# Attention block with a sine-gated feed-forward: batch 0's x by casting DMAs, and a new order of the opening

## The chip, the cores and the metric

The kernel runs on one core of one Trainium2 chip. The metric is the device time of one execution in microseconds, the median over several runs. TensorE is PE in the profile (PEld is its weight load), VectorE is DVE, ScalarE is ACT, GpSimd is POOL and SyncE is SP.

## The reference

```python
# x: (8, 8, 512, 64), state: (8, 8, 32, 64); scale = 1/sqrt(64)
a  = softmax(scale * x @ state^T)          # per batch and head: 512 x 32
xread = a @ state                          # 512 x 64
a2 = softmax(scale * state @ x^T)          # 32 x 512
sread = a2 @ x                             # 32 x 64
X  = concat([xread, sread], axis=2)        # -> (8 * 544, 512), heads side by side
h  = X @ w_in                              # 512 -> 2048
g  = h + sin(alpha * h)**2 / (alpha + 1e-9)
out = g @ w_out                            # 2048 -> 512, float32
```

Inputs and output are float32 in HBM; the matmuls run in bfloat16.

## The kernel before, in words

The 4352 rows of the output are cut into nine tiles: tile t = 0 to 7 holds the 512 xread rows of batch t, and tile 8 the 256 sread rows of all batches.

For tiles 0 to 7 the product `a @ state @ w_in` is regrouped: `M = state @ w_in` is made per batch (steps `m.b.s`, four column slices s of 512, each with two halves g), copied to bf16 by ACT or DVE (`me`), and multiplied with the transposed softmax weights `AT`. The 2048 hidden columns are 16 blocks f of 128. For each block, PE makes `h` (two matmuls of 512 columns, one for each g: `hg.t.f.g`, or `h.t.f` for both), ACT the sine (`si`), ACT, DVE or POOL its square (`sq`), DVE `gT = s2 / alpha + h` (`gt`), and PE adds gT into four output accumulators st = 0 to 3 (`o.t.st.f0.f1`). `oc` copies an accumulator out of PSUM, `os` stores it from SP.

The softmax weights of a batch come from: the load of x, its transpose xT, scores (`sc`), exponential (`ex`, ACT), row sums and reciprocals (`rs`, `rr`, DVE), the product `nm`, and a transpose of A into AT, by PE (`at`, `ac`) for batch 0 and by a DMA from SP (`ad`) for the later batches. Batch 1's x is transposed by PE (`xt`, `xc`), later ones by DMA (`td`); `pk` copies x into another layout, `xp`.

The order of every engine's work is written out by hand: `ORDER` is a list of steps, `name.arguments`, and each step issues its instructions on its engines in that order. The last numbers of a PE step are its PSUM banks; there are eight, and a step that takes a bank waits until the readers of what was in it are done. Every load of weights and of later batches' x (`li` = w_in slice, `lo` = w_out quarter, `l_st` = state, `lx` = x of a batch) is a DMA from POOL that casts float32 to bfloat16, in one queue. ACT changes its function table when it goes from exponential to sine and back.

The opening deals with batch 0: `lq.0` to `lq.3` load x in four float32 quarters from SP, `xq` casts them on ACT into xp, `xtq` transposes, `xc` copies to xT. Between these steps PE runs `warm_up.n.cols.bank`, matmuls on zeros whose result is not used. `st_t` and `st_c` transpose the state of batches 2 to 7, `s01_t` and `s01_k` that of batches 0 and 1, `al_t` the rows of alpha.

Of the kernel before, what the change touches and what calls it, by code (L numbers as in the profile page):

```python
# [12 lines left out]
BF16 = mybir.dt.bfloat16  # L13
FP32 = mybir.dt.float32
# [7 lines left out]
touch_x l_s01 consts touch lq.0.S ident_ l_alpha lq.1.S zero.0 warm_up.7.512.3 exp_table lq.2.S  # L22
zero.1 identf.V lq.3.S s01_c.G l_st li.0 xq.0.A s01_t.4 li.1 xtq.0.5 warm_up.1.384.3 xq.1.A
s01_k.1.V s01_k.0.A li.2 xtq.1.6 warm_up.2.448.3 xc.0.0.0.V xq.2.A xc.0.0.1.V lo.0 al_t.7 xq.3.A
xtq.2.0 warm_up.1.384.3 al_c inva sc.0.0.1 lo.1 xc.0.1.0.A warm_up.1.256.3 xtq.3.2 warm_up.2.128.3
ex.0.0 warm_up.2.128.4 lx.1.0.1 warm_up.2.128.5 xc.0.1.1.V warm_up.2.128.6 warm_up.2.128.7 rs.0.0
sc.0.1.0 li.3 st_t.0.3 ex.0.1 rr.0.0 st_t.1.4 lo.2 st_c.0.0.V st_c.0.1.A warm_up.2.128.5
warm_up.2.128.6 warm_up.2.128.1 st_c.1.0.A rs.0.1 warm_up.2.128.2 warm_up.2.128.7 nm.0.0.0.4.G
warm_up.2.128.0 warm_up.2.128.5 st_c.1.1.A warm_up.2.128.3 warm_up.2.128.6 warm_up.2.128.1 rr.0.1
warm_up.2.128.2 sin_table warm_up.2.128.7 warm_up.2.128.0 nm.0.1.0.4.G at.0.0.5 warm_up.2.128.3  # L30
ac.0.0.V m.0.0.6.4 m.1.0.1.2 lo.3 at.0.1.7 me.0.0.0.V me.0.0.1.A warm_up.2.128.0 warm_up.2.128.3
me.1.0.1.A ac.0.1.V hg.0.2.0.5 me.1.0.0.V hg.0.1.0.4 hg.0.2.1 hg.0.1.1 hg.0.0.0.0 lx.2.0.1 si.0.2
hg.0.0.1 m.1.1.6.3 si.0.1 m.0.1.7.2 hg.0.3.0.1 me.0.1.1.A sq.0.2.V hg.0.3.1 sq.0.1.G me.1.1.0.V
# [124 lines left out]
class Steps:  # L158
# [505 lines left out]
```

The softmax here doesn't subtract the row's maximum and nothing guards it: scores larger than these inputs give would overflow.

## Time and profile before

| what | us |
|---|---|
| median of 3 runs | 221.14 (220.92 to 221.36) |
| profiled execution (span) | 221.2 |
| PE busy | 215.7 (97%), of which 9.9 are warm-ups |
| ACT, DVE, POOL busy | 173.5, 162.4, 107.1 |
| first sine of tile 0 starts | 16.52 |
| step `h.1.8` starts on PE | 46.06 |

The span runs from the first to the last instruction of the core; the profiled execution agrees with the median within 0.1 us, so times read in the trace can be set against the runs directly. A busy PE in the table includes the modelled ends of pipelined matmuls; the distance from one start to the next is what counts in a stretch without gaps.

### The profile page before, as it was taken

How to read it: one execution, taken by the hardware profiler on the slowest of the kernel's cores; microseconds unless marked ns; L12 is line 12 of the kernel's file. 1: busy time of each engine (PE TensorE's matmuls, PEld its weight loads, DVE VectorE, ACT ScalarE, POOL GpSimd, SP SyncE). 2: the span in 40 equal slices, each digit the busy share in tenths (PEclk: the TensorE clock that was granted, in tenths of full speed). 3: DMA queues.
4: the chain of work that ended last, by engine and by line, in shares of the span. 5: the costliest groups of instructions: out<-in, count | busy, mean ns of one | idle time of the engine just before them, and what ended most of it. 6: DMA issues, size and time to landing. Idle time of an engine off the chain costs nothing.

```text
span 221.2 us, 4330 instructions
## 1 busy us (share of the span) xinstructions
PE 215.7 (97%) x1619; PEld 106.0 (48%) x1619; DVE 162.4 (73%) x286; ACT 173.5 (78%) x297; POOL 107.1 (48%) x115
## 2 busy tenths in 40 slices
PE   7999999999999999999999999999999999999994
PEld 3664454444444444444454444445445555665452
DVE  3468986999678979988888778889766988571201
ACT  3589878998899979998996999798857897685111
POOL 6866626595388728934863377363501072121000
PEclk9999999999999999999999999999999999999999
DMA  6999995953549518375325437380220211012042
GB/s 172 198 206 204 205 203 87 174 199 73 119 127 158 96 50 150 44 190 61 81 41 125 126 95 94 108 117 17 47 99 0 98 47 47 0 50 95 1 142 96
DMA packets 38052, 23.48 MB, mean 106 GB/s; under 512 B 20992, under 2 KB 33680, under 8 KB 38032
## 3 DMA queue, kind: packets, MB, share of 16 engines
q0 software_dynamic: 11648, 8.13, 26.1%
q1 hardware_dynamic: 26128, 15.08, 26.1%
q8 instruction: 12, 0.20, 0.4%
q14 instruction: 8, 0.07, 0.1%
q10 hardware_dynamic: 256, 0.01, 0.1%
HBM read 17.44 MB, written 8.91 MB: 119 GB/s over the span
## 4 chain that ended last, share of the span: by engine, by line
PE 93%; ACT 3%; DMA 2%; SPq 0%; issue 0%
PE o_ps L587 54%; PE h_ps L537 22%; PE m_ps L488 4%; PE h_ps L543 3%; PE h_ps L552 3%; DMA x<-in_x_dram 2%; PE s_ps L399 2%; PE warm_ps L303 2%; PE w_ps L450 2%; PE w_ps L461 1%; PE x_ps L361 1%; ACT L226 1%; ACT s L560 1%; ACT M L496 1%; PE x_ps L376 0%; PE st_ps L333 0%
## 5 line engine op out<-in xcount | busy, mean ns | idle before, releaser
L587 PE MATMUL o_ps<-w_out_sb,gT 128*128 128x512 bf16 (+2 forms) x560 | 137.7, 373 | 0.0
L576 DVE SCALAR_TENSOR_TENSOR gT<-s,inva_sb,h_ps 128x512 bf16<-128x512 bf16 (+1 forms) x144 | 96.6, 714 | 18.8 <-POOL s L201 9.6
L201 POOL TENSOR_TENSOR s<-s 128x512 bf16<-128x512 bf16 (+1 forms) x76 | 76.7, 1021 | 65.9 <-ACT s L560 62.4
L560 ACT ACTIVATE s<-h_ps,alpha_sb 128x512 bf16<-128x512 f32 (+1 forms) x144 | 88.8, 671 | 10.5 <-PE h_ps L543 4.3
L587 PEld LDWEIGHTS <-gT 128*128 128x128 bf16 x560 | 52.3, 98 | 60.3 <-issue 5.0
L537 PE MATMUL h_ps<-AT,M 128*128 128x512 bf16 x224 | 60.8, 379 | 0.0
L537 PEld LDWEIGHTS <-M 128*128 128x128 bf16 x224 | 21.7, 98 | 25.9 <-issue 0.4
L569 ACT ACTIVATE s<-s 128x512 bf16<-128x512 bf16 (+1 forms) x53 | 31.4, 595 | 0.8
L201 POOL TENSOR_TENSOR A<-E,rR 128x512 bf16<-128x512 bf16 x16 | 16.6, 1048 | 25.7 <-ACT o_sb L595 12.7
L595 ACT COPY o_sb<-o_ps 128x512 f32<-128x512 f32 (+2 forms) x24 | 13.7, 571 | 16.6 <-PE o_ps L587 16.5
L496 ACT CAST M<-m_ps 128x512 bf16<-128x512 f32 x35 | 18.6, 594 | 8.2 <-PE m_ps L488 8.1
L496 DVE CAST M<-m_ps 128x512 bf16<-128x512 f32 x29 | 18.9, 679 | 2.5 <-PE m_ps L488 2.1
L595 DVE COPY o_sb<-o_ps 128x512 f32<-128x512 f32 x11 | 7.6, 691 | 13.0 <-PE o_ps L587 12.9
L303 PE MATMUL warm_ps<-warm 128*128 128x128 bf16 (+3 forms) x66 | 9.9, 295 | 1.4 <-DVE warm L209 1.2
L410 DVE TENSOR_REDUCE R<-E 128x16 f32<-128x512 bf16 x16 | 10.4, 658 | 1.1 <-ACT E L406 0.9
L201 DVE TENSOR_TENSOR s<-s 128x512 bf16<-128x512 bf16 (+1 forms) x15 | 6.2, 415 | 6.8 <-ACT s L560 6.7
L488 PE MATMUL m_ps<-w_in_sb,stT 64*32 64x512 bf16 x256 | 10.2, 382 | 0.0
L468 DVE RECIPROCAL rC<-w_ps 128x128 f32<-128x128 f32 x8 | 7.6, 948 | 3.2 <-PE w_ps L461 3.2
L406 ACT ACTIVATE E<-s_ps 128x512 bf16<-128x512 f32 x16 | 8.8, 601 | 1.4 <-PE s_ps L399 1.3
L552 PE MATMUL h_ps<-AT,M 128*128 128x512 bf16 x32 | 9.4, 380 | 0.4 <-ACT M L496 0.4
L543 PE MATMUL h_ps<-xs_all,w_in_sb 128*128 128x256 bf16 x64 | 9.1, 273 | 0.0
L560 ACT ACT_TABLE_LOAD x5 | 6.4, 1283 | 2.2 <-PE h_ps L537 1.1
(56 smaller groups left out, 104.3 us busy)
## 6 DMA issues: line engine op xcount, KB each, us to landing
out_dram<-o_sb SPq DMA_DIRECT2D x33, 256.0 KB, 2.3
xnat<-in_x_dram POOLq DMA_DIRECT2D x7, 512.0 KB, 7.7
w_in_sb<-in_moe_w_in_dram POOLq DMA_DIRECT2D x4, 512.0 KB, 10.3
w_out_sb<-in_moe_w_out_dram POOLq DMA_DIRECT2D x4, 512.0 KB, 16.3
x<-in_x_dram SPq DMA_DIRECT2D x4, 256.0 KB, 4.3
st_nat<-in_state_dram POOLq DMA_DIRECT2D x1, 256.0 KB, 5.7
out_dram<-o_sb SPq DMA_DIRECT2D x1, 192.0 KB, 1.9
s<-in_state_dram SPq DMA_DIRECT2D x1, 128.0 KB, 2.1
```

What stands on the lines that cost most here:

```text
L201: {"V": k.nc.vector, "G": k.nc.gpsimd}[eng].tensor_tensor(out, a, b, ALU.mult)
L303: k.nc.tensor.matmul(wp[:, :cols], k.warm[:, 0:k.P], k.warm[:, :cols], start=True, stop=True)
L488: k.nc.tensor.matmul(k.t["m", b, s + n, g][o0:o0 + k.Ns, :], k.stT[k.half(r), b * k.G + g, c0:c0 + k.Ns], k.w_in_sb[k.half(r), 2 * g + h, ...
L496: k.copy(eng)(k.t["M", b][:, g, s * k.FW:(s + 1) * k.FW], k.t["m", b, s, g][:])
L537: k.nc.tensor.matmul(hp[:, :n], k.t["M", t][:, g, fs], k.t["AT", t][:, g, :], start=(g == 0), stop=(g == k.G - 1),)
L543: k.nc.tensor.matmul(hp[:, :n], k.w_in_sb[:, q, fs], k.xs_all[:, q].rearrange("p b j -> p (b j)"), start=(q == 0), stop=(q == k.Q - 1),)
L552: k.nc.tensor.matmul(k.t["h", t, f][:], k.t["M", t][:, g, f * k.P:(f + 1) * k.P], k.t["AT", t][:, g, :], start=(g == 0), stop=(g == k.G - 1),)
L560: k.nc.scalar.activation(s[:, :n], k.t["h", t, f][:, :n], ACT.Sin, scale=k.alpha_sb[:, f:f + 1])
L569: k.nc.scalar.activation(s2[:, :n], s[:, :n], ACT.Square)
L576: k.nc.vector.scalar_tensor_tensor(gT[:, :n], k.t["s2", t, f][:, :n], k.inva_sb[:, f:f + 1], k.t["h", t, f][:, :n], ALU.mult, ALU.add,)
L587: k.nc.tensor.matmul(k.t["o", t, st, half][:, cols], k.t["gT", t, f][:, rows], k.w_out_sb[:, f, cols], start=(f == 0), stop=(f == k.FT - 1),)
L595: k.copy(eng)(o_sb[:, cols], k.t["o", t, st, half][:, cols])
```

## The change

Of batch 0's x, only the first quarter (heads 0 and 1, `lq.0`) is still loaded in float32 from SP; DVE casts it into the bf16 tile `xnat` (`xn.0`). The other three quarters come as two casting DMAs, the first instructions of POOL's queue: `lx.0.1.4` (heads 2 and 3) and `lx.0.1.2` (heads 4 to 7), ahead of POOL's identity matrix. `xth` transposes x from `xnat` in halves of 64 columns, and xp of batch 0 is made by `pk` on DVE. The loads in POOL's queue stand in the order x0, x0, w_in 0, w_in 1, w_out 0, state, x1, w_in 2, w_out 1, w_in 3, w_out 2, x2, w_out 3; before it was state, w_in 0, 1, 2, w_out 0, 1, x1, w_in 3, w_out 2, 3, x2. The first 312 steps stand in a new order, with 11 warm-up matmuls in place of 66: tile 0's blocks come as f = 0, 1, 2 and so on, batch 0's two `nm` go from POOL to DVE, `s01_c` from POOL to DVE, and `st_t`/`st_c` come after the first `hg` blocks. From `h.1.8` on, the order is that of before with the banks renamed one for one. `hg` now starts an accumulation where a bank is given.

```diff
--- before
+++ after
 ORDER:
-touch_x l_s01 consts touch lq.0.S ident_ l_alpha lq.1.S zero.0 warm_up.7.512.3 exp_table lq.2.S
-zero.1 identf.V lq.3.S s01_c.G l_st li.0 xq.0.A s01_t.4 li.1 xtq.0.5 warm_up.1.384.3 xq.1.A
-s01_k.1.V s01_k.0.A li.2 xtq.1.6 warm_up.2.448.3 xc.0.0.0.V xq.2.A xc.0.0.1.V lo.0 al_t.7 xq.3.A
-xtq.2.0 warm_up.1.384.3 al_c inva sc.0.0.1 lo.1 xc.0.1.0.A warm_up.1.256.3 xtq.3.2 warm_up.2.128.3
-ex.0.0 warm_up.2.128.4 lx.1.0.1 warm_up.2.128.5 xc.0.1.1.V warm_up.2.128.6 warm_up.2.128.7 rs.0.0
-sc.0.1.0 li.3 st_t.0.3 ex.0.1 rr.0.0 st_t.1.4 lo.2 st_c.0.0.V st_c.0.1.A warm_up.2.128.5
-warm_up.2.128.6 warm_up.2.128.1 st_c.1.0.A rs.0.1 warm_up.2.128.2 warm_up.2.128.7 nm.0.0.0.4.G
-warm_up.2.128.0 warm_up.2.128.5 st_c.1.1.A warm_up.2.128.3 warm_up.2.128.6 warm_up.2.128.1 rr.0.1
-warm_up.2.128.2 sin_table warm_up.2.128.7 warm_up.2.128.0 nm.0.1.0.4.G at.0.0.5 warm_up.2.128.3
-ac.0.0.V m.0.0.6.4 m.1.0.1.2 lo.3 at.0.1.7 me.0.0.0.V me.0.0.1.A warm_up.2.128.0 warm_up.2.128.3
-me.1.0.1.A ac.0.1.V hg.0.2.0.5 me.1.0.0.V hg.0.1.0.4 hg.0.2.1 hg.0.1.1 hg.0.0.0.0 lx.2.0.1 si.0.2
-hg.0.0.1 m.1.1.6.3 si.0.1 m.0.1.7.2 hg.0.3.0.1 me.0.1.1.A sq.0.2.V hg.0.3.1 sq.0.1.G me.1.1.0.V
-me.1.1.1.A warm_up.2.128.2 gt.0.2 si.0.0 warm_up.2.128.2 warm_up.2.128.6 warm_up.2.128.3
-warm_up.2.128.2 warm_up.2.128.6 me.0.1.0.A gt.0.1 sq.0.0.G m.0.2.3.2 si.0.3 m.1.2.5.6 hg.0.4.0.7
 ...
-si.1.13 h.1.15.2 sq.1.3.G gt.1.6 os.0.1 o.0.2.15.16 oc.0.0.A h.1.5.4 sq.1.13.G oc.0.2.V si.1.15
-h.1.7.3 os.0.0 gt.1.3 o.1.1.0.1.5 si.1.5 os.0.2 h.1.8.1 sq.1.15.G gt.1.13 o.1.1.1.2 si.1.7
-o.1.2.0.2.7 sq.1.5.A o.1.1.2.3 sq.1.7.G h.1.12.0 gt.1.15 si.1.8 h.1.9.6 gt.1.5 o.1.2.2.3 si.1.12
 ...
+l_s01 lx.0.1.4 touch_x consts lq.0.S touch zero.0 lx.0.1.2 l_alpha exp_table zero.1 ident_ li.0
+identf.V s01_c.V warm_up.4.512.7 warm_up.1.256.6 s01_t.0 li.1 xn.0.V al_t.1 s01_k.1.A s01_k.0.V lo.0
+xth.0.0.2 al_c inva xth.0.1.3 l_st xc.0.0.0.A xc.0.0.1.A lx.1.0.1 warm_up.1.512.0 xth.0.2.4
+xth.0.3.5 li.2 xc.0.1.0.A pk.0.0.V sc.0.0.6 xc.0.1.1.A pk.0.1.V lo.1 ex.0.0 warm_up.1.224.3 sc.0.1.7
+li.3 rs.0.0 ex.0.1 m.0.0.0.1 lo.2 sin_table rr.0.0 rs.0.1 nm.0.0.0.4.V me.0.0.0.A rr.0.1
+warm_up.3.512.6 warm_up.1.320.7 at.0.0.2 nm.0.1.0.4.V me.0.0.1.A m.0.1.3.4 ac.0.0.V at.0.1.5
+me.0.1.1.A me.0.1.0.V hg.0.0.0.6 m.1.0.7.0 ac.0.1.V m.1.1.1.2 me.1.0.1.A me.1.0.0.V hg.0.1.0.4
+hg.0.0.1 me.1.1.0.A hg.0.1.1 me.1.1.1.V hg.0.2.0.3 si.0.0 hg.0.2.1 hg.0.3.0.5 lx.2.0.1 hg.0.3.1
+si.0.1 sq.0.0.V hg.0.4.0.0 hg.0.4.1 si.0.2 gt.0.0 hg.0.5.0.7 lo.3 hg.0.5.1 st_t.0.1 si.0.3 sq.0.1.V
+sq.0.2.G st_t.1.2 si.0.4 gt.0.1 hg.0.6.0.6 st_c.0.0.A st_c.0.1.V hg.0.6.1 sq.0.3.G st_c.1.0.A
+o.0.0.0.1.4 gt.0.2 o.0.0.1.2 st_c.1.1.A hg.0.7.0.1 hg.0.7.1 si.0.5 pk.1.0.V sq.0.4.G xt.1.1.2 gt.0.3
+si.0.6 xt.1.0.3 si.0.7 xc.1.1.0.V sq.0.5.G o.0.0.2.3 gt.0.4 o.0.1.0.1.5 xc.1.1.1.A o.0.1.1.2
+o.0.1.2.3 xc.1.0.0.V sq.0.6.G xc.1.0.1.A o.0.0.3.4 sc.1.1.0 gt.0.5 sq.0.7.A o.0.2.0.1.2 sc.1.0.3
+o.0.2.1.2 pk.1.1.V ex.1.1 o.0.3.0.1.7 gt.0.6 o.0.3.1.2 o.0.2.2.3 o.0.3.2.3 gt.0.7 o.0.1.3.4
+o.0.2.3.4 o.0.3.3.4 m.0.2.6.1 ex.1.0 rs.1.1 o.0.0.4.5 me.0.2.0.A o.0.1.4.5 me.0.2.1.V m.1.2.0.3
+o.0.2.4.5 me.1.2.1.A hg.0.8.0.6 me.1.2.0.V hg.0.8.1 hg.0.9.0.1 si.0.8 hg.0.9.1 rs.1.0 hg.0.10.0.3
+hg.0.10.1 rr.1.1 hg.0.11.0.0 rr.1.0 hg.0.11.1 nm.1.1.0.4.G o.0.3.4.5 o.0.0.5.6 o.0.1.5.6 o.0.2.5.6
+si.0.9 o.0.3.5.6 lx.3.0.1 sq.0.8.V o.0.0.6.7 o.0.1.6.7 si.0.10 gt.0.8 o.0.2.6.7 o.0.3.6.7
+nm.1.0.0.4.G si.0.11 o.0.0.7.8 sq.0.9.V o.0.1.7.8 o.0.2.7.8 sq.0.10.V o.0.3.7.8 sq.0.11.A gt.0.9
+o.0.0.8.9 ad.1 o.0.1.8.9 o.0.2.8.9 gt.0.10 o.0.3.8.9 m.0.3.6.1 o.0.0.9.10 gt.0.11 me.0.3.0.A
+o.0.1.9.10 o.0.2.9.10 me.0.3.1.A o.0.3.9.10 pk.2.0.V m.1.3.3.6 pk.2.1.V hg.0.12.0.0 me.1.3.0.A
+hg.0.12.1 me.1.3.1.V hg.0.13.0.1 td.2 si.0.12 hg.0.13.1 hg.0.14.0.3 hg.0.14.1 si.0.13 hg.0.15.0.6
+sq.0.12.G hg.0.15.1 o.0.0.10.11 si.0.14 o.0.1.10.11 sq.0.13.V o.0.2.10.11 si.0.15 o.0.3.10.11
+gt.0.13 o.0.0.11.12 sq.0.14.G o.0.1.11.12 o.0.2.11.12 gt.0.12 sq.0.15.A hg.1.0.0.1 hg.1.0.1
+o.0.3.11.12 gt.0.14 si.1.0 hg.1.1.0.0 hg.1.1.1 o.0.0.12.13 gt.0.15 si.1.1 hg.1.2.0.3 sq.1.0.G
+hg.1.2.1 o.0.1.12.13 si.1.2 o.0.2.12.13 sq.1.1.V hg.1.3.0.6 hg.1.3.1 gt.1.1 o.0.3.12.13 sq.1.2.A
+o.0.0.13.14 o.0.1.13.14 gt.1.0 si.1.3 o.0.2.13.14 hg.1.4.0.0 hg.1.4.1 gt.1.2 o.0.3.13.14 sq.1.3.G
+si.1.4 hg.1.5.0.1 hg.1.5.1 o.0.0.14.15 si.1.5 hg.1.6.0.3 sq.1.4.V hg.1.6.1 gt.1.3 o.0.1.14.15 si.1.6
+o.0.2.14.15 o.0.3.14.15 o.0.0.15.16 gt.1.4 hg.1.7.0.6 sq.1.6.G oc.0.0.A hg.1.7.1 o.0.1.15.16
+hg.1.13.0.0 os.0.0 oc.0.1.A hg.1.13.1 hg.1.15.0.4 gt.1.6 hg.1.15.1 si.1.13 os.0.1 o.0.2.15.16
+o.0.3.15.16 si.1.15 oc.0.2.V o.1.1.0.1.5 sq.1.13.G oc.0.3.A os.0.2 os.0.3 h.1.8.3 sq.1.15.G gt.1.13
+o.1.1.1.2 si.1.7 o.1.2.0.2.2 sq.1.5.A o.1.1.2.3 sq.1.7.G h.1.12.7 gt.1.15 si.1.8 h.1.9.0 gt.1.5
 ...
...
     def lq(k, q, eng):
-        if q == 0:
-            k.x0 = k.const.tile([k.P, k.H, k.C * k.D], FP32, name="x0")
         hs = slice(2 * q, 2 * q + 2)
+        k.t["x0", q] = k.const.tile([k.P, 2, k.C * k.D], FP32, name=f"x0_{q}")
...
+    def xn(k, q, eng):
+        xnat = k.new(0, "xnat", k.xpool, [k.P, k.H, k.C * k.D], BF16)
+        k.copy(eng)(xnat[:, 2 * q:2 * q + 2, :], k.t["x0", q][:])
...
     def lx(k, b, part, parts):
-        if part == 0:
-            k.t["xnat", b] = k.xpool.tile([k.P, k.H, k.C * k.D], BF16, name="xnat")
+        xnat = k.new(b, "xnat", k.xpool, [k.P, k.H, k.C * k.D], BF16)
         hs = slice(part * k.H // parts, (part + 1) * k.H // parts)
...
-    def xq(k, q, eng):
-        xp = k.new(0, "xp", k.xppool, [k.P, k.C, k.H, k.D], BF16)
-        hs = slice(2 * q, 2 * q + 2)
-        k.copy(eng)(xp[:, :, hs, :], k.x0[:, hs, :].rearrange("p h (i d) -> p i h d", i=k.C))
-
-    def xtq(k, q, bank):
-        tp = k.t["xtq", q] = k.ps(bank, [k.P, k.S], BF16, "x_ps")
+    def xth(k, b, q, bank):
+        tp = k.t["xth", b, q] = k.ps(bank, [k.P, k.S], BF16, "x_ps")
         for i in range(k.C):
-            k.nc.tensor.transpose(tp[:, i * k.P:(i + 1) * k.P], k.pair(0, i, q), k.ident[:])
+            for r in range(2):
+                k.nc.tensor.transpose(
+                    tp[k.half(r), i * k.P:(i + 1) * k.P],
+                    k.t["xnat", b][:, 2 * q + r, i * k.D:(i + 1) * k.D],
+                    k.ident[:],
+                )
...
     def hg(k, t, f, g, *bank):
-        if g == 0:
+        if bank:
...
-            start=(g == 0), stop=(g == k.G - 1),
+            start=bool(bank), stop=not bank,
```

## The prediction

> **What bounds the kernel now.** I read the busy shares first, then the stretches of the span, then the opening in the timeline, then the DMA landings. The stretches (columns: stretch, PE busy and count, PEld, DVE, ACT, POOL, granted clock, DMA share, GB/s):
>
> ```profile
> 16.00:19.40 3.40, 3.17 (x43) 1.37 (x42) 2.15 (x4) 3.21 (x7) 1.04 (x1) 1.00 1.24 206
> 19.40:24.00 4.60, 4.60 (x36) 2.07 (x36) 4.45 (x8) 4.60 (x10) 4.29 (x5) 1.00 1.37 201
> 24.00:46.00 22.00, 22.00 (x156) 10.37 (x154) 18.80 (x34) 18.84 (x31) 11.67 (x12) 1.00 1.08 177
> 46.00:100.00 54.00, 54.00 (x399) 24.69 (x397) 45.93 (x80) 49.06 (x84) 35.11 (x36) 1.00 0.55 113
> 100.00:218.00 118.00, 118.00 (x848) 58.74 (x846) 83.01 (x143) 88.02 (x154) 43.39 (x44) 1.00 0.30 72
> ```
>
> From 19.4 us to 218 us PE never stands still, and in that stretch one 512-column matmul starts every 0.216 us. So every useful matmul that PE has done when it becomes gap-free brings the end forward, and every later gap puts it back. Before 19.4, PE's busy time is mostly filler:
>
> ```profile
> L303 PE MATMUL warm_ps<-warm 128*128 128x128 bf16 (+3 forms) x66 | 9.9, 295 | 1.4 <-DVE warm L209 1.2 <-ACT M L496 0.2
> ```
>
> That is PE's group of warm-ups up to 19.4. The opening's chain in the timeline (start, duration, what):
>
> ```profile
> 4.36 0.62 ACT L356 CAST xp<-x 128x512 bf16<-128x512 f32 x1 [0.69 <-DMA x<-in_x_dram]
> ...
> 8.68 0.64 PE L399 MATMUL s_ps<-stT,xT 128*128 128x64 bf16 x8
> ...
> 10.66 0.40 PE L399 MATMUL s_ps<-stT,xT 128*128 128x64 bf16 x8
> ...
> 11.10 0.60 ACT L406 ACTIVATE E<-s_ps 128x512 bf16<-128x512 f32 x1 [1.15 <-PE s_ps L399]
> ...
> 13.24 1.05 POOL L201 TENSOR_TENSOR A<-E,rR 128x512 bf16<-128x512 bf16 x1 [0.74 <-DVE rR L416]
> ...
> 13.73 1.28 ACT L226 ACT_TABLE_LOAD   x1
> ...
> 16.52 1.26 ACT L560 ACTIVATE s<-h_ps,alpha_sb 128x512 bf16<-128x512 f32 x2 [0.19 <-PE h_ps L552]
> ```
>
> x lands in quarters, ACT casts each, the second exponential ends at 11.7, POOL's second product at 14.29, the first sine starts at 16.52. The two equal groups of s_ps also show PE's rate: 0.64 us at 8.7, 0.40 at 10.7. PE runs at half rate until about 10.5, though the granted clock reads 1.00.
>
> After step `h.1.8` the two orders are the same (banks renamed one for one). Before starts it at 46.06 in the timeline; the end moves by what that start moves. The profiled execution takes 221.2 us, as the median of 221.14, so I subtract from 221.2.
>
> **The landing of x.** Removed: three fp32 quarters on SP and four ACT casts of 0.62. Added: two casting DMAs at the head of POOL's queue, a DVE cast `xn` (0.4 to 0.7 by the 128x512 rows) and two DVE copies `pk.0` (0.42 each, in DVE's wait for the first exponential). The x transposes become 32 of half width instead of 16: eight such took PE 0.64 in the state's group, four whole ones 0.61, so they are even. POOL can issue from 0.74; the two issues take some 0.75 each and push `ident_` to about 2.8, covered by the fillers until 3.2. No row shows this queue used first with a bf16 target of 256 KB, so bounds: the state load of 256 KB, first on the queue before, landed 5.7 after issue; the 512 KB xnat loads landed 5.9 to 8.0 after theirs:
>
> ```profile
> xnat<-in_x_dram POOLq DMA_DIRECT2D x1, 512.0 KB, 8.0
> ```
>
> Queued loads landed every 2.55 us per 512 KB (w_in at 11.6, 14.1, 16.7), 205 GB/s. The state row plus 128 KB (0.6) gives 0.74+5.7+0.6 = 7.05; the xnat rows less 128 KB (0.6) give 6.0 to 8.1. I take 7.05, the row nearest in place and size. Then w_in 0 lands at 9.6, w_in 1 at 12.1, w_out 0 at 14.7, the state at 16.0, x of batch 1 at 18.5, w_in 2 at 21, w_out 1 at 23.6, w_in 3 at 26, w_out 2 at 29.
>
> The Trainium skill, "DMA: Bandwidth & Descriptors", section "Anatomy of one DMA", gives such a load about 2 us plus its bytes at 436 GB/s; by that estimate x would be there before 5 us and the sum below would fall by 0.4 more, where `alpha` takes over. The trace's 5.7 for the state load disagrees, and the sum goes by the trace.
>
> **The chain to the first hidden tile** (durations from the rows; PE at half rate). `al_t` now stands ahead of x on PE; alpha rows landed at 5.2, so `xth.0` 5.3, `xth.1` 5.75. `xth.2` 7.05 to 7.7, `xth.3` to 8.15. ACT: four xT copies 5.95 to 8.8. `sc.0.1` 8.85 to 9.5, second exponential 9.5 to 10.1 (before: 11.7). Sine table 1.5, to 11.6; first M copies to 12.7. DVE: sums 0.68, reciprocals 0.25, and the two `nm` that move from POOL (1.05) to DVE. No row shows that product on DVE; the bf16 one there takes 0.42, POOL's 1.05; I take 0.65, near the 0.68 of rows that read fp32. That ends `nm` at 12.55 (before 14.29). PE: `m.0.0` at 9.6, fillers to 11.65, `at.0.0`, `m.0.1` at 12.15 (w_in 1 at 12.1), `at.0.1` 12.6 to 13.05. First `hg` 13.05 (before 15.11). ACT's five M copies end at 15.2; first sine 15.25 against 16.52.
>
> **From there to h.1.8.** PE work left: 117 matmuls of 512 columns x 0.216 = 25.3; six `m` x 0.3 = 1.8; `st_t` 0.9, `xt` 0.85, `sc` 0.5. Sum 29.35, so 42.4 without a stop. Stops, following ACT (sines every 0.6): sines 0 to 4 until 18.3, three `st_c` (1.46, now here instead of ahead of the tile) until 19.75, sines 5 to 7 until 21.6, xT copies to 22.65, a square to 23.25, exp table 1.28, two exponentials to 25.65, two M copies, sine table to 28.0.
> - half rate until about 14.3: 0.65;
> - `o.0.0` waits for DVE's `gt.0.1` (18.1): 0.05;
> - `hg.0.7` waits for its bank until `st_c` at 18.8: 0.25;
> - `xt.1.1` waits for the last `st_c` at 19.75: 0.5;
> - `sc.1.1`, `sc.1.0` wait for xT copies: 0.5;
> - `m.1.2` waits for the second exponential of batch 1 at 25.65: 0.25.
>
> Sum 2.2: `h.1.8` at 44.6 instead of 46.06, **1.45 us earlier**. The sine table load (to 28.0) is covered: 8 `hg` and 13 `o` (4.5 us) carry PE from 26.2 until tile 0's f=8 is needed at 30.7, and its gT is ready at 29.8. Without that cover it would cost 1.3. Loads have 1 to 7 us: x of batch 1 needed at 19.8, w_out 1 at 25, w_out 2 at 30.7, w_out 3 (31.9) at 37. On POOL, `lx.3` (0.94) stands between batch 1's two `nm` and holds the second to 30.6; `ad.1` (about 3.2 to land) then comes at 34, needed at 36.3. The 55 warm-ups fewer cost PE nothing where it waits anyway.
>
> Forecast: 221.2 - 1.45 = 219.75, rounded to 219.8.
>
> **The clock.** In the trace the half rate ends near 10.5, after a stretch from 7 us nearly full with fillers, transposes and scores. In the new order the same density comes with `m.0.0` and the long fillers at 9.6, hence full rate near 14.3. "TensorE: Matmul & The Clock Gate" in the Trainium skill ("What's actually happening" and Part 4) wants a busy window of about 3.4 us and says that transposes do not count; it speaks against dropping fillers. By it full rate would come only at 16.5 to 19.5 and the sum would lose up to 1.5 us of its gain. No row here separates transposes from fillers. From the trace alone: if half rate lasts to the `o` at 18, eleven `hg` cost 0.216 more each, 2.4 us, of which PE's 1.2 of waits up to 19.8 absorb half: h.1.8 at 45.8, 220.9.
>
> **Rivals.**
> 1. The lead is given back (no change, 220.7 to 221.6). Either the clock case above, or DVE: tile 0's f=8 to 11 are squared on DVE (0.42) with gT (0.66 each), PE reaches `m.0.3` at 31.6 and its bank 1 comes free at 31.2. With DVE 1 us later, PE waits 0.6 there and some again at `hg.0.12`. For: DVE is 97% busy at 19.4 to 24 before. Against: the table of batch 1 comes 3 us earlier than before, so ACT's later stretch is looser.
> 2. Slower: the software queue's first load lands late. From `xth.2` to the first sine each us of lateness is a us of time, w_in 0 and 1 with it. Landing at 8.5 (7.05+1.45) cancels the gain; beyond 8.95 it is measurably slower. For: first packets of this queue before moved only after SP's x; 8.0 from issue is a row. Against: SP now has a third of the bytes ahead. At 9.2, 0.5 past the largest xnat row's 8.7 from 0.74, the time is 221.9.
> 3. The DMA cast brings nothing, since `alpha` or ACT's order holds the chain anyhow: an earlier landing than 6.65 gains no more; then 219.4, the low side.
>
> **How the numbers follow.** Forecast case 0.64 (own range 219.0 to 220.6: landing 6.0 to 7.9 gives -0.4 to +0.8, two `nm` on DVE of 0.42 to 1.05 each give -0.45 to +0.8, not all at once). Given back 0.17, slower 0.19. Range 218.9 to 221.8. 0.2%, 0.44 us, is about what a measurement of this kernel can tell from no change: faster is below 220.7, slower above 221.58. The forecast case reaches 220.6, so faster 0.64, same 0.17, slower 0.19.
>
> **What would show it.** Right: xnat's second load lands at 6 to 8, first sine near 15.3, `h.1.8`'s L537-type matmul near 44.6, PE full from 26 on. Wrong: PE waits for ACT or DVE after 26; 512-column matmuls 0.43 apart after 15; w_in waits at `m.0.1`; or a first xnat landing past 8.5.

## The result, and the profile after

The changed kernel is slower: 229.19 us (median of four runs, 227.61 to 233.19) against 221.03, a ratio of 1.034 [1.028, 1.040]. A second set gave 229.84 against 221.2, 1.037 [1.030, 1.044]. The longest runs, from 232 us up, count as slow executions: they are in the medians and left out of the ratios. The forecast was 219.8, with 221.8 as its upper end.

The profiled execution of after took 227.61 us and has a span of 225.2. The stretches, with the columns as before (us, PE busy and count, PEld, DVE, ACT, POOL, granted clock, DMA share, GB/s):

```profile
16.00:19.40 3.40, 3.40 (x44) 1.83 (x43) 2.69 (x5) 3.40 (x8) 1.65 (x3) 1.00 1.39 202
19.40:24.00 4.60, 4.12 (x51) 2.11 (x50) 4.46 (x8) 3.73 (x8) 4.10 (x4) 1.00 1.24 206
24.00:46.00 22.00, 21.41 (x127) 8.79 (x127) 18.74 (x32) 18.89 (x30) 7.71 (x8) 1.00 0.97 150
46.00:100.00 54.00, 52.24 (x387) 23.58 (x386) 45.45 (x76) 47.23 (x81) 34.35 (x35) 1.00 0.59 113
```

PE was never idle after 19.4 in before. Now this view shows it idle for 0.48, 0.59 and 1.76 us in the last three stretches, most of it after 46 us, where the order of steps is that of before. The view counts the modelled ends of the matmuls as busy; measured from one start to the next, the time lost in stops is larger: 1.36 (19.4 to 24), 0.8 (24 to 46) and 2.3 (46 to 100). What PE waited for from 19 to 100 us (total, times, longest):

```profile
PE s_ps L399 <- DVE gT L576: 1.1, 2, 0.8
PE h_ps L537 <- DVE gT L576: 1.0, 1, 1.0
PE o_ps L587 <- DVE gT L576: 0.3, 1, 0.3
PE h_ps L552 <- DVE gT L576: 0.2, 1, 0.2
```

For before the same view has no line. The chain that ended last, by engine, says the same (before: PE 93%):

```profile
PE 76%; DVE 7%; DMA 7%; ACT 6%; POOL 2%; issue 1%; POOLq 0%
```

The warm-ups are 11 instead of 66, and the opening in the timeline is this (start, duration):

```profile
8.81 0.63 PE L399 MATMUL s_ps<-stT,xT 128*128 128x64 bf16 x8
8.87 1.21 ACT L406 ACTIVATE E<-s_ps 128x512 bf16<-128x512 f32 x2
10.29 0.63 PE L488 MATMUL m_ps<-w_in_sb,stT 64*32 64x512 bf16 x8 [0.84 <-DMA w_in_sb<-in_moe_w_in_dram]
10.85 1.73 PE L304 MATMUL warm_ps<-warm 128*128 128x512 bf16 x4
11.82 0.69 DVE L200 TENSOR_TENSOR A<-E,rR 128x512 bf16<-128x512 bf16 x1
12.37 0.63 PE L430 MATMUL a_ps<-ident,A 128*128 128x128 bf16 x4
16.14 1.28 ACT L560 ACTIVATE s<-h_ps,alpha_sb 128x512 bf16<-128x512 f32 x2
```

The second exponential ends at 10.08, as forecast (10.1). The score groups still take 0.63, PE's half rate, which lasts until 15.53. w_in 0 lands at 10.24 and holds `m.0.0`; the four fillers behind it (1.73 us at half rate) hold the transpose of A until 12.37, although its product was ready at 11.62. The first sine starts at 16.14.

**The profile shown of before was of an execution some 2 us longer than the runs.** The 13 runs of before in the second set have spans of 218.8 to 220.9, and their time is 1.9 us more than their span; by that distance the profile's 221.2 would belong to an execution of about 223. A profile of a typical one (`before_again`, span 219.3, time 221.24) shows the difference in the same places:

```profile
8.34 0.41 PE L399 MATMUL s_ps<-stT,xT 128*128 128x64 bf16 x8
8.79 0.60 ACT L406 ACTIVATE E<-s_ps 128x512 bf16<-128x512 f32 x1 [0.37 <-PE s_ps L399]
14.35 1.26 ACT L560 ACTIVATE s<-h_ps,alpha_sb 128x512 bf16<-128x512 f32 x2 [0.19 <-PE h_ps L552]
```

Full rate comes at 4.86 instead of 10.49, the second exponential ends at 9.39 instead of 11.70, the first sine starts at 14.35 instead of 16.52. So this table compares after with before's order in `old_open_new_tail` below, whose record is complete (us from the span's start):

| point | before's order | after | `no_collisions` |
|---|---|---|---|
| PE at full rate from | 7.02 | 15.53 | 15.81 |
| second exponential ends | 9.84 | 10.08 | 10.18 |
| first sine of tile 0 | 14.67 | 16.14 | 16.35 |
| first output matmul of tile 1 (just ahead of `h.1.8`) | 44.00 | 47.24 | 46.20 |
| first score of batch 2 | 49.18 | 53.42 | 51.47 |
| last matmul | 216.03 | 221.62 | 218.75 |
| span, time of that run | 219.3, 221.23 | 225.2, 227.61 | 222.3, 224.76 |

After loses 1.5 up to the first sine, 1.8 from there to tile 1, 2.3 behind it and 0.3 after the last matmul. Another 0.5 lies outside the span: time less span is 1.9 for before's order and 2.4 to 2.5 for after and `no_collisions`. It is 2.2 in `x_only`, 2.1 in `order_only` and 2.0 to 2.1 in `nc_x_sp` below, so most of the 0.5 goes with the casting loads of x; why, no run here shows.

### The profile page after: what moved, and what is told of

It is laid out like the page before. It is cut to its first block, busy times and chain, and to the rows that moved or that the text cites. A ratio compares the mean times of both kernels' runs of the same rounds, so it can differ in the third digit from the quotient of the medians.

```text
span 225.2 us, 4246 instructions
## 1 busy us (share of the span) xinstructions
PE 215.7 (96%) x1580; PEld 102.8 (46%) x1580; DVE 166.2 (74%) x290; ACT 174.2 (77%) x298; POOL 103.5 (46%) x111
## 4 chain that ended last, share of the span: by engine, by line
PE 76%; DVE 7%; DMA 7%; ACT 6%; POOL 2%; issue 1%; POOLq 0%
PE o_ps L587 45%; PE h_ps L537 16%; PE m_ps L488 4%; DMA xnat<-in_x_dram 4%; DVE gT L576 4%; PE h_ps L543 3%; DMA w_in_sb<-in_moe_w_in_dram 3%; PE h_ps L552 2%; ACT s L560 2%; ACT M L496 2%; PE w_ps L450 2%; DVE xp L348 2%; PE s_ps L399 1%; DVE s L200 1%; PE w_ps L461 1%
## 5 line engine op out<-in xcount | busy, mean ns | idle before, releaser
L200 POOL TENSOR_TENSOR s<-s 128x512 bf16<-128x512 bf16 (+1 forms) x73 | 73.8, 1025 | 68.1 <-ACT s L560 66.8
L537 PEld LDWEIGHTS <-M 128*128 128x128 bf16 x204 | 19.8, 98 | 24.8 <-issue 1.9
L496 ACT CAST M<-m_ps 128x512 bf16<-128x512 f32 x39 | 20.8, 591 | 12.8 <-PE m_ps L488 12.7
L569 ACT ACTIVATE s<-s 128x512 bf16<-128x512 bf16 (+1 forms) x50 | 29.3, 589 | 0.8
L595 ACT COPY o_sb<-o_ps 128x512 f32<-128x512 f32 (+2 forms) x25 | 14.3, 572 | 17.1 <-PE o_ps L587 16.8
L200 POOL TENSOR_TENSOR A<-E,rR 128x512 bf16<-128x512 bf16 x14 | 14.5, 1048 | 27.6 <-ACT o_sb L595 12.9
L496 DVE CAST M<-m_ps 128x512 bf16<-128x512 f32 x25 | 16.3, 678 | 2.9 <-PE m_ps L488 2.8
L200 DVE TENSOR_TENSOR s<-s 128x512 bf16<-128x512 bf16 (+1 forms) x21 | 10.3, 493 | 7.8 <-ACT s L560 7.6
L488 PE MATMUL m_ps<-w_in_sb,stT 64*32 64x512 bf16 x256 | 11.8, 411 | 1.0 <-DMA w_in_sb<-in_moe_w_in_dram 0.8
L348 DVE COPY xp<-xnat 128x1024 bf16<-128x1024 bf16 x16 | 8.5, 557 | 2.3 <-DMA xnat<-in_x_dram 2.3
L276 POOL DMA_DIRECT2D xnat<-in_x_dram x9 | 8.1, 905 | 2.6 <-DMA w_in_sb<-in_moe_w_in_dram 1.8
## 6 DMA issues: line engine op xcount, KB each, us to landing
w_in_sb<-in_moe_w_in_dram POOLq DMA_DIRECT2D x4, 512.0 KB, 11.6
```

Source lines behind the costliest of these rows:

```text
L200: {"V": k.nc.vector, "G": k.nc.gpsimd}[eng].tensor_tensor(out, a, b, ALU.mult)
L348: k.copy(eng)(k.t["xp", b][:, :, hs, :], k.t["xnat", b][:, hs, :].rearrange("p h (i d) -> p i h d", i=k.C),)
L488: k.nc.tensor.matmul(k.t["m", b, s + n, g][o0:o0 + k.Ns, :], k.stT[k.half(r), b * k.G + g, c0:c0 + k.Ns], k.w_in_sb[k.half(r), 2 * g + h, ...
L496: k.copy(eng)(k.t["M", b][:, g, s * k.FW:(s + 1) * k.FW], k.t["m", b, s, g][:])
L537: k.nc.tensor.matmul(hp[:, :n], k.t["M", t][:, g, fs], k.t["AT", t][:, g, :], start=(g == 0), stop=(g == k.G - 1),)
L569: k.nc.scalar.activation(s2[:, :n], s[:, :n], ACT.Square)
```

## The experiments

**Which part costs.** One repeat of after, and three kernels with the change undone in part.

`again`: no edit.

> The changed kernel once more, unchanged. Its runs spread from 227.6 to 233.2 us where those of before stay within 0.8. If the cost sits in DVE copies that start while a POOL product is running (0.42 us becomes up to 1.28), which copies are hit depends on a few tenths of a microsecond, so a second profile shows a different set of stretched copies and a time anywhere from 227 to 233. If the cost is a fixed consequence of the order, the second profile has its gaps at the same steps, within 0.1 us, and the same 225.2 us span.

229.84. The stretched copies are the same as in after, within 0.04 us in length: not chance, but consequence of the order. The new thing is PE's stop ahead of tile 1, 0.38 us in after and 1.08 here, now put down to a DMA (what PE waited for, 19 to 100 us, the three longest):

```profile
PE s_ps L399 <- DVE gT L576: 1.1, 2, 0.8
PE h_ps L537 <- DVE gT L576: 1.0, 1, 1.0
PE h_ps L552 <- DMA AT<-A: 0.9, 1, 0.9
```

`x_only`, on before:

```diff
-touch_x l_s01 consts touch lq.0.S ident_ l_alpha lq.1.S zero.0
+l_s01 lx.0.1.4 touch_x consts lq.0.S touch zero.0 lx.0.1.2 l_alpha ident_
...
-xq.0.A
+xn.0.A
...
-xtq.0.5
+xth.0.0.5
...
-xc.0.1.1.V
+xc.0.1.1.V pk.0.0.V pk.0.1.V
```

`lq.1` to `lq.3` and `xq.1` to `xq.3` are left out, and the other three `xtq` become `xth` likewise.

> Before's order and fillers, and only batch 0's x loaded by the two casting DMAs at the head of POOL's queue (the state and the weights behind them in the order of before). If the new order is what costs, this is within 1.5 us of before (219.5 to 222.5; the second x load lands at 7.1 to 7.2, the second exponential ends about 10.5 instead of 11.7, but w_in 0 lands at 12.8 instead of 11.6 and takes the lead back). If the casting loads are what costs, this is 225 or more.

225.60, 1.019 [1.015, 1.024]: slower by itself, as the second reading had it. In its profile the state lands at 9.58 instead of 8.76 and the first sine comes 0.48 later; 1.68 more is one stop at batch 4's score, whose DMA transpose took 5.9 us instead of 4.3. The profile is of the shortest run (223.88); the others took 225.3 to 226.2, and what they lose beyond it has no trace.

What ran beside that transpose, the trace shows (queues and issues from 70 to 78 us):

```profile
q8 instruction: 1, 0.02, 0.7%
xT<-xp SPq DMA_TRANSPOSE x1, 5.9
```

The same transpose in `old_open_new_tail` below, whose window has no packet of that queue:

```profile
xT<-xp SPq DMA_TRANSPOSE x1, 4.3
```

All 20 traces say the same. Of 131 DMA transposes issued with no casting load in flight, 24 took 0.85 to 1.64 us longer than usual, and in each of the 24 a 16 KB packet of the queue listed as `q8 instruction` starts 1.0 to 3.9 us after the issue. The 99 with no such packet were within 0.3 of the usual, and so were the 8 in which it came only in the first 0.15 or the last 0.3 us. No run moved that packet, so this is a coincidence in time and not a cause shown. The 1.68 cannot be put down to the casting loads themselves.

`order_only`, on after:

```diff
-l_s01 lx.0.1.4 touch_x consts lq.0.S touch zero.0 lx.0.1.2
+l_s01 touch_x consts lq.0.S touch lq.1.S zero.0 lq.2.S lq.3.S
...
-xth.0.1.3 l_st xc.0.0.0.A
+xn.1.A xth.0.1.3 l_st xn.2.A xn.3.A xc.0.0.0.A
```

> The changed kernel with x loaded as before: four fp32 quarters from SP, cast by DVE (first) and ACT (three, 0.6 each); order, fillers and POOL's other loads as in the changed kernel. If the new order is what costs, this stays at 226 to 231. If the loads of x ahead of w_in are what costs, w_in 0 lands about 2.5 us earlier (7.5 to 8) and the time comes back to 219 to 222.

234.75, 1.061 [1.058, 1.065], worse than the changed kernel and outside both readings. POOL's w_in loads now start at 1.43 and share the DMA engines with SP's quarters, which land at 5.4, 9.3 and 11.6 (6.7 for the last in before's order, where POOL starts at 3.3). The four, and the two w_in loads issued beside them:

```profile
x<-in_x_dram SPq DMA_DIRECT2D x4, 256.0 KB, 7.1
w_in_sb<-in_moe_w_in_dram POOLq DMA_DIRECT2D x2, 512.0 KB, 8.6
```

`old_open_new_tail`: before's steps up to `h.1.8`, with banks 0 to 7 become 7, 3, 4, 6, 1, 5, 0, 2, and after's steps from there.

```diff
-os.0.2 h.1.8.1 sq.1.15.G gt.1.13
+os.0.2 h.1.8.3 sq.1.15.G gt.1.13
```

> The steps of before up to h.1.8 (banks renamed) and from there, word for word, the changed kernel's steps. If the changed kernel's loss after h.1.8 comes from the moment at which it arrives there, this is before again: 221.0 within 0.5. If the banks named anew in the rest of the order cost something, it is 222.5 to 224.5, with the gaps that the changed kernel has at sc.2 and at pk.4.

221.25, 1.000 [0.998, 1.003]. The renaming is free; what after loses behind `h.1.8` depends on when and in what state it gets there. So the casting loads cost 4.4 us in before's order (`x_only`), and the new order on top of them 4.2 more (229.84 against 225.60).

**Three candidates, each alone and together**, on after.

`fillers`:

```diff
-warm_up.4.512.7
+warm_up.6.512.7
...
-warm_up.1.512.0
+warm_up.3.512.0
...
-sc.0.1.7
+sc.0.1.7 warm_up.4.512.2
...
-warm_up.3.512.6
+warm_up.6.512.6
```

> The changed kernel with 11 more 512-column fillers on PE in the opening (two more at the start, two more ahead of the second half of x, four between the scores and w_in 0, three more ahead of the transposes of A). If PE's half rate until 15.5 us holds the opening back, full rate now comes at 7 to 10, the first sine at 14.8 to 15.4 instead of 16.14, the first output matmul of tile 1 about 1 us earlier than 47.24, and the time is 1 to 2 us under the changed kernel's 229. If the half rate only fills waits, the first sine stays at 16.0 to 16.5 and the time at 228 to 231; fillers in the way of the transposes would make it later still.

230.45, 1.044 [1.040, 1.048]. Full rate came at 4.14, yet the first sine only at 15.84: w_in 0 landed at 10.90 and the fillers kept the transpose of A until 12.72. PE then stopped 1.8 ahead of tile 1.

`lx4_early`:

```diff
-sq.1.14.G
+sq.1.14.G lx.4.0.1
...
-h.2.3.2 lx.4.0.1 ad.3
+h.2.3.2 ad.3
```

> The changed kernel with the load of batch 4's x moved up in POOL's queue, from 66.1 us to POOL's idle time at 54.6. If PE's stop at 75.7 comes from that load (issued 66.09, landed 74.71, DVE waits 1.43 for it ahead of three gT), the load lands near 63 and the time falls by 1.1 to 1.5; if the load is also what spreads the runs by 5 us (a stop long enough lets the clock drop), the runs now lie within 1.5 us. If the spread comes from the opening, it stays at 4 to 5 us, and only the 1.1 to 1.5 go. If DVE's copy was slow for its own reasons, nothing changes.

229.87, 1.039 [1.035, 1.043]. The stop at 75.7 went (1.13), and a new one came at batch 3's score: its DMA transpose, issued just behind the moved load, took 8.1 us instead of 4.3.

```profile
PE s_ps L398 <- DMA xT<-xp: 1.9, 1, 1.9
```

`pk3_late`:

```diff
-sq.1.12.A pk.3.1.V
+sq.1.12.A
...
-pk.3.0.V
+pk.3.0.V pk.3.1.V
```

> The changed kernel with the copy pk.3.1 on DVE moved from ahead of three gT (51.45, 1.26 us while POOL multiplies) to right behind pk.3.0, where POOL's product ends as DVE gets there. If a DVE copy that starts during a POOL product waits for that product's end, the copy takes 0.42 again, PE's stop of 0.91 at 53 shrinks to under 0.3 and the time falls by 0.5 to 0.9. If the copy's 1.26 us has nothing to do with POOL, it is 0.8 us or more at the new place too and the time stays.

230.25, 1.038 [1.032, 1.045]. PE's stop at 53 (0.91) is gone, but the copy is 1.26 long again: it started 0.24 into a POOL product that ended at 57.37, and ended itself at 57.65. In this run the clock shows what a longer stop does. Stretches around it (PE, PEld, DVE, ACT, POOL, granted clock, DMA, GB/s):

```profile
77.80:81.34 3.54, 1.47 (x7) 0.58 (x6) 3.54 (x5) 1.88 (x4) 2.51 (x3) 1.00 0.15 31
81.34:84.75 3.41, 3.41 (x9) 1.18 (x8) 3.41 (x6) 2.74 (x4) 1.04 (x1) 0.50 0.65 122
84.75:88.00 3.25, 3.25 (x50) 2.12 (x49) 0.53 (x2) 1.09 (x2) 0.00 (x0) 1.00 0.02 5
```

PE stood for 2.2 us at 77.8; the granted clock then read 0.50 for 3.41 us, in which 512-column matmuls start every 0.427 instead of 0.216 us: 1.7 us lost. `order_only` (3.4 us stop) and `all_three` (2.8) show the same; stops of 1.7 to 1.8 (`fillers`, `before_lx3_early`, `x_only`) and one of 2.05 (`lx4_early`) don't. After's runs above 228.5 have a mean clock of 0.985 or 0.993 in three of four cases, the size of two and of one such window. They left no trace, so it is likely, and not shown, that the spread of its runs comes in part from stops near this limit.

`all_three`: the edits of `fillers`, `lx4_early` and `pk3_late` in one.

```diff
+warm_up.6.512.7
...
+pk.3.0.V pk.3.1.V
...
+sq.1.14.G lx.4.0.1
```

> The fillers, the early load of batch 4's x and the late pk.3.1 together, in the changed kernel. If the three causes are separate, the gains add up: 3 to 5 us under the changed kernel, 224.5 to 226.5, with runs within 2 us. What is then left above the 221.2 of before is the chain from the first sine to tile 1, 31.1 us in the changed kernel and 29.3 in before. If they stand for one cause, the sum is no more than the largest of the three.

230.80, 1.042 [1.039, 1.046]. The gains did not add: ad.1 at 40.1, batch 3's transpose 8.4 us, a stop of 2.8, a window at half rate.

**The DMA transposes.** ad.1, the DMA transpose of batch 1's A, takes another time in each kernel. Two kernels move the load of batch 3's x past it; the issues (KB, us to landing) around it in before, after and the two follow behind the edits.

`lx3_late`, on after:

```diff
-o.0.3.5.6 lx.3.0.1 sq.0.8.V
+o.0.3.5.6 sq.0.8.V
...
-sq.0.14.G
+sq.0.14.G lx.3.0.1
```

> The changed kernel with the load of batch 3's x moved back in POOL's queue, from between the two products of batch 1 (30.45 us) to after batch 1's transpose of A has landed (about 39). If that load is what makes the DMA transpose ad.1 take 6.5 to 8.0 us (3.1 to 3.3 in before, where the load comes after it), ad.1 is issued 0.9 earlier, lands by 35.5, PE's stop ahead of tile 1's first hidden block (0.4 to 1.8 us, at 38.5) is gone, and the time is 1 to 2 us under the changed kernel's 229 to 230. If the weights still in flight (w_out 3 until 35) delay it, ad.1 still takes 5 us or more and the time stays.

`before_lx3_early`, on before:

```diff
-nm.1.0.0.4.G
+lx.3.0.1 nm.1.0.0.4.G
...
-td.2 si.1.2 lx.3.0.1 h.1.0.2
+td.2 si.1.2 h.1.0.2
```

> Before's kernel with one load moved: batch 3's x ahead of batch 1's first product on POOL, as in the changed kernel (there right ahead of the second). If a load just ahead of a DMA transpose holds it up, ad.1 takes 6 to 8 us instead of 3.2, lands at 40 to 42, PE stops 2 to 5 us ahead of tile 1's first hidden block, and the time is 223.5 to 226. If the queues do not meet, it is 221.2 to 222 (POOL's product 0.94 later, with 1.5 us to spare).

Before:

```profile
AT<-A SPq DMA_TRANSPOSE x1, 3.2
```

After (the load at 30.45, the transpose at 32.50):

```profile
xnat<-in_x_dram POOLq DMA_DIRECT2D x1, 512.0 KB, 7.7
AT<-A SPq DMA_TRANSPOSE x1, 6.5
```

`lx3_late`:

```profile
AT<-A SPq DMA_TRANSPOSE x1, 4.6
```

`before_lx3_early`, its two issues and what PE waited for:

```profile
xnat<-in_x_dram POOLq DMA_DIRECT2D x1, 512.0 KB, 10.1
AT<-A SPq DMA_TRANSPOSE x1, 5.7
```

```profile
PE h_ps L536 <- DMA AT<-A: 1.6, 1, 1.6
```

In after ad.1 landed 0.8 us behind that load, in `before_lx3_early` 1.1. The same load moved costs 1.9 us in before (223.32, 1.010 [1.006, 1.014]); moved in after, it gives back 2.4 to 3.1 (226.75, 1.026 [1.020, 1.031]). There ad.1 lands at 36.4, 4.6 us after its issue and not 3.2, since weight and x loads issued before it were still landing. The stops at 33 and 75.7 went too; DVE's square and copy there no longer met a POOL product (0.49 for 1.28 at 31.6).

`pk1_late`, on after:

```diff
-si.0.5 pk.1.0.V
+si.0.5
...
-pk.1.1.V ex.1.1
+ex.1.1
...
-gt.0.7
+gt.0.7 pk.1.0.V pk.1.1.V
```

> The changed kernel with DVE's two copies of batch 1's x (20.77, 0.84 us beside a POOL product, and 24.16, 0.41) moved out of the run of gT from 19.5 to 26 to behind gt.0.7, where DVE waits. If DVE's queue is what stops PE between 19.6 and 24.3 (1.4 us in four stops), 0.8 to 1.2 us of these go, the first output matmul of tile 1 comes as much earlier, unless the transpose of batch 1's A (landing at 39 to 40) takes it all back: then PE's stop at 38.5 grows by the same amount and the time does not move. If ACT's copies are what PE waits for, the stops stay.

228.17, 1.032 [1.027, 1.037]. The stops between 19.6 and 24.3 fell from 1.4 to 0.5; ad.1 (6.7 us) took part of it back.

`no_collisions`: the edits of `lx3_late`, `pk1_late` and `pk3_late`, and batch 4's load in a new place.

```diff
-h.2.3.2 lx.4.0.1
+h.2.3.2
...
-sq.1.6.G
+sq.1.6.G lx.4.0.1
```

> The changed kernel with the four moves that take copies and transfers out of each other's way: batch 3's x after ad.1, batch 4's x at about 46 (ahead of the DMA transpose td.3 and done before it), pk.3.1 behind pk.3.0, and batch 1's copies behind gt.0.7. If the losses are these collisions, ad.1 takes 3.1 to 3.3, td.3 4.3, no stop of PE over 0.5 us is left after 25 us, the clock stays up, and the time is 224 to 226.5, within 1.5 us from run to run. What is left over 221.2 is the opening. If the losses come back in other places, as the earlier load of batch 4's x gave its gain back at sc.3, it is 228 or more.

224.68, 1.014 [1.010, 1.018], runs of 223.54 to 225.23. The clock stayed at 1.00 and td.3 took 4.3, as expected; ad.1 did not take the 3.1 to 3.3 expected but 5.6 (it landed at 36.8, the last weight load at 35.7), which cost PE only 0.38. All that the view of PE's waits lists between 19 and 100 us:

```profile
PE o_ps L586 <- DVE gT L575: 0.3, 1, 0.3
PE h_ps L551 <- DVE gT L575: 0.2, 1, 0.2
```

From start to start, four stops of 0.26 to 0.42 are left. So four places in the order hold 4.5 to 5.2 of the 8.2 to 8.6 us. pk.3.1 is still 1.27 long; it now costs 0.4.

**The rest: the opening.** All on `no_collisions`, but for `x_only_lx4`.

`nc_rate`:

```diff
-warm_up.4.512.7
+warm_up.6.512.7
...
-warm_up.1.512.0
+warm_up.3.512.0
...
-sc.0.1.7
+sc.0.1.7 warm_up.3.512.2
...
-warm_up.3.512.6
+warm_up.2.512.6
```

> The version without collisions (224.7) with fillers where PE waits: two more of 512 columns at the start, two more ahead of the second half of x, three between the scores and w_in 0, and one less ahead of the transposes of A. If half rate and the fillers in the way hold the opening back, full rate comes at 4 to 8 us, the transposes of A start at 11.9 to 12.1 instead of 12.57, the first sine at 15.0 to 15.5 instead of 16.35, and the time is 223.2 to 224. If w_in 0 and w_in 1 (landing 10.4 and 13.0) hold it, the first sine stays at 16.0 or later and the time at 224.5 to 225.5.

`nc_rate_li0`, on nc_rate:

```diff
-ident_ li.0
+li.0 ident_
```

> The same, with the first w_in load issued ahead of POOL's identity matrix (about 2.9 instead of 3.44). If w_in's landing holds the opening, w_in 0 and all loads behind it land 0.4 to 0.6 earlier and the time is 0.3 to 0.6 under the version before it; the identity, 0.8 later, delays the transposes of the state by under 0.5 and is covered by x's landing at 7.2. If the queue's rate and not its start sets the landing, nothing changes (within 0.3).

225.54, 1.019 [1.015, 1.024], and 225.41, 1.018 [1.015, 1.022]: no gain. Full rate came at 9.06 and 4.46, the transposes of A at 12.09 and 11.73, the first sine at 15.8 and 15.7 only; batch 2's ad.2 then took 4.4 and 4.3 instead of 3.1 and stopped PE 1.4 and 1.3, in both with an instruction packet beside it as in `x_only`. So what the earlier full rate is worth by itself is not shown. The earlier issue of w_in 0 did not bring its landing forward (10.87, 10.76).

`nc_rate_m1`, on nc_rate:

```diff
-m.0.1.3.4 ac.0.0.V at.0.1.5 me.0.1.1.A me.0.1.0.V hg.0.0.0.6
+ac.0.0.V at.0.1.5 hg.0.0.0.6
...
-hg.0.3.1
+hg.0.3.1 m.0.1.1.2 me.0.1.1.A me.0.1.0.V
...
-hg.0.5.1
+hg.0.5.1 m.1.1.1.2 me.1.1.0.A me.1.1.1.V
```

> nc_rate (225.5) with the two products that need w_in 1 (m.0.1 and m.1.1) and their copies moved behind the hidden blocks that do not need them. If the wait for w_in 1 ahead of the second transpose of A sets the first sine, at.0.1 starts at 12.5 to 12.8 instead of behind m.0.1 (13.4 or later), the first sine at 14.2 to 14.8 instead of 15.8, and the time is 0.4 to 1.2 us lower. If ACT's and DVE's total work from 13 to 26 us sets the pace, the first sine comes earlier but tile 1 does not, and the time is within 0.3 of nc_rate.

226.62, 1.023 [1.020, 1.026]. Its profile is a poor test of the first part. It is of the longest run (228.39); w_in 0 landed at 11.65 and the clock fell to 0.50 from 12.1 to 15.5 (first sine 16.04). The moved products then stopped PE for 1.8 us between 17 and 20, behind ACT's and DVE's copies. What sets the first sine is not settled by it.

`nc_x_sp`, on no_collisions:

```diff
-l_s01 lx.0.1.4 touch_x consts lq.0.S touch zero.0 lx.0.1.2
+l_s01 touch_x consts lq.0.S touch ident_ lq.1.S zero.0 lq.2.S lq.3.S
...
-ident_ li.0 identf.V s01_c.V
+identf.V s01_c.G li.0
...
-xth.0.1.3 l_st xc.0.0.0.A xc.0.0.1.A
+xn.1.A xth.0.1.3 l_st xn.2.A xn.3.A xc.0.0.0.V xc.0.0.1.V
```

In the steps behind `li.2`, `sc.0.0.6` also comes ahead of `pk.0.0.V`, and `xc.0.1.1` goes from ACT to DVE.

> The version without collisions with x loaded as in before: four fp32 quarters from SP, cast by DVE (first) and ACT (three), and POOL's other loads held until about 3.3 by the identity and the state's cast on POOL, as in before. If the casting loads bring nothing, x lands by 6.7, the second exponential ends at 9.8 to 10.6, w_in 0 lands at 9 to 10.5, and the time is within 1 us of 224.7. If they are worth what the two new-order kernels without and with them differ by (234.75 and 229.8), it is 228 or more.

224.43, 1.014 [1.009, 1.020]: the casting loads of x bring nothing that these runs can tell, in this order. With SP's quarters ahead of POOL's loads the second exponential ends at 9.57, with the casting loads at 10.18; w_in 0 lands at 10.64 and 10.44.

`x_only_lx4`, on x_only:

```diff
-td.2 si.1.2 lx.3.0.1
+td.2 si.1.2 lx.3.0.1 lx.4.0.1
...
-h.2.3.7 lx.4.0.1
+h.2.3.7
```

> Before's order with the casting loads of x (225.6), and batch 4's x loaded right behind batch 3's at about 35 instead of 62. If the casting loads cost by way of the chain load, copy, DMA transpose, score of batch 4, which had no slack in before (xT landed 75.07, score at 75.13), the stop of 1.68 us at that score is gone and the time is 221.4 to 223. If they cost by themselves, it stays at 225 or more. A new stop at batch 2's score (its DMA transpose is issued while two loads are in flight, needed at 49.5) would show as a landing after 49.5.

224.02, 1.013 [1.009, 1.016]: 1.6 back, not all. Batch 4's DMA transpose still takes 5.9 us with its load long landed, and again an instruction packet starts during it (74.88). So moving the load could not have removed this delay if the packet goes with it; whether it does is untested.

`before_again`: no edit.

> Before's kernel, unchanged. Its runs have spans of 218.8 to 220.9, so this profile should show a span near 219.3, full rate from 4.5 to 7.1 us instead of 10.5, the second exponential's end near 9.8 instead of 11.7 and the first sine near 14.7 instead of 16.5.

As expected (above). No version here beats before; the best of the new order is 1.4% behind it.

## Why the prediction was wrong, step by step

- **"The profiled execution takes 221.2 us, as the median of 221.14, so I subtract from 221.2."** This failed first. Span and time are different things (1.9 us apart), and their agreement was chance. Half rate until 10.49 belonged to that execution. Against a typical one there was no 1.6 us to gain at the second exponential: before's order ends it at 9.4 to 9.8, the new one at 10.1. A typical one starts `h.1.8` at 44.2 (`old_open_new_tail`), so even the forecast's own 44.6 would have been 0.4 late. The Trainium skill, "TensorE: Matmul & The Clock Gate", section "What's actually happening", says that the window of 3413 ns runs freely and that the change comes at another point from run to run, by 500 ns either way. The traces agree on the window (3.41 us of half rate at a time) but not on the size: in before's order full rate came from 4.7 to 10.5 us, a spread of 5.8, and the measurement decides. I cited that page for the new order and did not turn it on the profile that I subtracted from.
- **The landing of x** held: 7.18 for 7.05. w_in 0 was 0.6 late (10.24 for 9.6), and this term was mis-sized: the next load came 3.06 us after x's, not 2.55.
- **The chain to the first sine**, 15.25, came at 16.14: half rate lasted until 15.53, not 14.3, and the fillers that were costed at nothing stood ahead of a transpose that was ready.
- **From there to h.1.8.** The stops at 19.4 to 24, put at 1.25, were 1.36; that term was right. Two others were missing. "`ad.1` (about 3.2 to land)" took 6.5 in after and 7.2 in `again`. I had counted `lx.3` as 0.94 on POOL's queue, but not its 512 KB in the DMA engines that the transpose needs. The trace of before had shown it: its ad.4, issued at 83.58, 0.1 after a load of x, took 6.8 us. And DVE's copies and squares were taken at 0.42 throughout.
- **"After step h.1.8 the two orders are the same; the end moves by what that start moves."** It moved by 2.3 more to the last matmul, and 0.3 behind it. Equal order gives equal time only while nothing waits. Before's order has little slack on the chain load, copy, DMA transpose, score of batch 4 (in `old_open_new_tail` xT landed at 75.07, the score started at 75.13), and DVE's copies of batch 3's x start there when a product of POOL has at most a tenth of a microsecond left. In before, DVE and POOL stand like this (start, duration; POOL's nine products follow without a gap):

```profile
49.41 0.42 DVE L348 COPY xp<-xnat 128x1024 bf16<-128x1024 bf16 x1
51.72 0.42 DVE L348 COPY xp<-xnat 128x1024 bf16<-128x1024 bf16 x1
```

```profile
43.36 9.68 POOL L201 TENSOR_TENSOR s<-s 128x512 bf16<-128x512 bf16 x9 [0.19 <-ACT s L560]
```

In after like this:

```profile
51.45 1.26 DVE L348 COPY xp<-xnat 128x1024 bf16<-128x1024 bf16 x1
54.60 0.41 DVE L348 COPY xp<-xnat 128x1024 bf16<-128x1024 bf16 x1
```

```profile
48.40 6.21 POOL L200 TENSOR_TENSOR s<-s 128x512 bf16<-128x512 bf16 x6
```

The product that the first copy met here ended at 52.43, almost 1 us after the copy started.

- **The rivals.** Slower, by the landing of the software queue's first load: right sign, wrong mechanism (it landed on time). "The DMA cast brings nothing": `nc_x_sp` agrees, for the order of `no_collisions`; the reason given, `alpha` or ACT, was not tested. The lead given back by the clock and by DVE's chain: both were there, and my price for them, ending at no change, was too low. The base was 1.9 off, and neither ad.1's delay nor the 2.3 behind `h.1.8` was in it.
- **The whole miss.** 229.2 against 219.8 is 9.4: `h.1.8` at 47.46 for 44.6 (2.9), the stretch from there to the end (2.6), time less span (2.4, of which 1.9 was before's too), and 1.6 by which the median of after lies above the run that was profiled.

## What to carry to other kernels

Check a profile's span against the spans of many runs before you subtract from it, above all in an opening where PE's rate may differ from run to run. In a schedule written out by hand, two things that no engine's queue shows decide whether a moved step is free: which loads were issued ahead of a DMA transpose and are still landing, and whether POOL is multiplying when a bf16 copy on DVE starts. An order without idle time on PE may have no slack on several chains, and then being late at one point is paid again later.

## What was not expected of the hardware

- In 20 traces, 113 DVE copies or squares in bf16 started while a POOL product had 0.05 us or more to run; every one ended 0.28 to 0.37 us after that product's end (up to 1.28 us long). Of 583 others (28 of them in the last 0.04 us of a product), all but eight took at most 0.47, and those eight (0.56 to 0.80) ran in the first 10 us, while POOL was issuing DMAs. The Trainium skill, "SBUF — State Buffer", section "SBUF: two separate sides", calls the port pair of the two engines an exclusive lock held for a whole instruction; the traces agree.
- DMA transposes took 3.0 to 3.3 us (A) and 4.2 to 4.4 (xT) with little else in flight. A casting load issued before them and still landing delays them. Transposes of x took 5.0 to 8.8 where it landed 2.3 us or more after their issue, and 4.2 to 4.5 where it landed within 1.5. ad.1 landed 0.4 to 1.3 us after the last load issued before it in 19 of 20 traces (in `before` none was in flight): where that load landed within 2.3 us of ad.1's issue, ad.1 took its usual 3.1 to 3.4, and where it landed 2.8 to 7.6 after, 3.8 to 8.0. A load issued 0.9 us after ad.1 (five traces) left it at 3.1 to 3.4.
- With no load in flight, some took 0.85 to 1.64 us more, each time with a packet of the queue `q8 instruction` beside them (above, under `x_only`).
- In PE's busy stream, a stop of 2.2 us or more was followed by 3.41 us at a granted clock of 0.50; stops up to 2.05 were not. In the opening of `nc_rate_m1` a wait of about 1.5 us came before such a window, so the limit holds for the stream only.
- With eight loads in flight in POOL's queue, the ninth waited until the first of these had landed (w_out 2, issued 10.53, for w_in 0, landed 10.24, and two more like it). Whether the queue or a wait of the program's own holds it, no run shows. It cost nothing here.
